# Attention and two mixture layers in one kernel: sixth unit multiplied as loaded, w_out decoded into PSUM and its logits taken from the split parts

## The chip, the core and the metric

One core of one Trainium2 chip. The metric is the device time of one execution in microseconds (us). The kernel before took 819.07 us, the median of three runs (817.53 to 819.14).

## What is computed

Sparse attention over 4 batches of 8 heads, 768 positions of 64 (a window of 128 and four leading positions), then a dense layer with a softmax-weighted activation and a layer norm, then a gated layer in which each of the 3,072 tokens goes to one of eight experts. Cut to what bears on the change:

```python
x = attn_out.transpose(0, 2, 1, 3).reshape(B * S, H * D)
h = x @ w_in
sm = softmax(h)
solu = h * sm
ln = (solu - mu) / np.sqrt(var + 1e-06) * g_ln
x2 = ln @ w_out
logits = x2 @ w_gate
expert_idx = argmax(logits); out = gate_w * (relu(x2 @ w1[e]) @ w2[e])
```

The inputs come in double precision as far as `w_in` and `w_out` are concerned: the kernel receives them as pairs of 32-bit words and makes float32 out of them itself.

## The kernel before, in words

All matrix products that need more than the short multiplication format are made from two parts: a high part (float32r, rounded by the write) and a low part (the value less its high part), so that a product takes three matmuls of one pass, or two where one side is exact.

**Attention** (`a_load`, `a_split`, `a_scores`, `a_sinks`, `a_trans`, `a_out`) runs over 32 units; a unit is two heads by 384 positions. Units 0 to 4 (`n < NATP`, NATP = 5) are multiplied as loaded: L225 multiplies float32 q and k of 64 rows directly. From unit 5 on, `a_split` makes high and low parts first: ScalarE copies k and q (L190, L191), GpSimd subtracts (L192, L193), and nine transfers on SyncE's queue (L198) stack high and low parts in the 128 rows; L228 and L229 then multiply. For each of six score tiles VectorE applies the mask and takes the maximum (L232, L233) and ScalarE the exponential (L235). The score tiles `s`, the sink tiles `skp` and, for later units, `tp` and `av` share three PSUM banks (tag "psa", PA = 3); everything else shares the other five ("psm").

**Weights** (`load_w_in`, `load_w_out`, both through `decode`) come in 16 chunks, eight of each matrix. ScalarE turns the low words into numbers (L350), VectorE joins the words in two operations (L351 into a PSUM tile `dt`, L352 into the result), ScalarE makes the high part (L362 or L397) and VectorE the low part (L363 or L398). For `w_in` the result of L352 is a PSUM tile `dh`; for `w_out` it is the SBUF tile `dec`. Each chunk of `w_out` also gives the gate's logits columns: TensorE transposes the decoded chunk in four pieces (L376), ScalarE copies it to `xt` (L378), TensorE multiplies by the gate's weights (L384, 8 columns), and VectorE writes the eight result columns behind the chunk's 512 (L387, L388). At step k of the loop the product of chunk k-2 stands ahead of the transposes of chunk k-1.

**Dense layer** (`m_in`, `m_act`, `m_tr`, `m_out`, `m_route`) runs over 24 blocks of 128 tokens. `m_in` multiplies by `w_in` (L453 to L455, 512 columns) and needs the outputs `bxh`, `bxl` (L311, L312) of four units, the first four for block 0.

**Order.** The program writes the steps in an order of its own: attention alone until the first four units are out, then attention and dense layer in a proportion (RATIO) of their estimated PE times, which the `yield` values give. The loading of weights is one step for each entry of `W_AT`: entry i says after which exponential step i comes. What is left of it is run through before the first `m_out` ("wo"). From this written order a scheduler sets each engine's own order; every engine then works its list strictly from the top.

```python
            if last2:
                logits2(*last2)
                last2 = None
            if last:
                last2 = logits(*last)
            last = (k, x)
            yield 1.5
```

Of the kernel before, what the change touches and what calls it, by code (L numbers as in the profile page):

```python
# [8 lines left out]
F32 = mybir.dt.float32  # L9
F32R = mybir.dt.float32r  # L10
BF16 = mybir.dt.bfloat16
I32 = mybir.dt.int32
U32 = mybir.dt.uint32
AF = mybir.ActivationFunctionType
ALU = mybir.AluOpType
# [14 lines left out]
NPT, XBUFS, QKB, PKB, VB = 2, 8, 2, 2, 2  # L30
WB, DB, EB, NXR, XGB = 4, 4, 2, 2, 6
PA = 3
NATP, LEAD = 5, 4
KLV = 2
LA = 2
TE = 18
# [1 line left out]
XT = 21  # L38
WSB = 6
HG, HD, HSTEP, FH = 1, 5, 2, 1  # L40
W_AT, RATIO = [1, 4, 7, 10, 13, 16, 19, 22, 24, 26, 27, 29, 30, 32, 33, 35], 0.7
ROOM = [608, 576, 512, 416, 384, 320, 288, 128]
CAPS = [-(-n // 128) * 128 for n in ROOM]
NBLK = sum(CAPS) // 128
# [4 lines left out]
SC_IN, SC_OUT, SX = 2.0 ** 8, 2.0 ** 64, 2.0 ** -8  # L49
# [3 lines left out]
def raw(ap):  # L53
    return ap.bitcast(F32)
# [3 lines left out]
def body(ctx, tc, a):  # L58
    nc = tc.nc
    V, A, G, T, SY = nc.vector, nc.scalar, nc.gpsimd, nc.tensor, nc.sync  # L60
# [3 lines left out]
    const = ctx.enter_context(tc.tile_pool(name="const", bufs=1))  # L64
# [18 lines left out]
    def ps(name):  # L83
        if name in ATT:
            a_ = True
        elif name in MOE:
            a_ = False
        else:
            flip[0] += 1
            a_ = flip[0] % 8 < PA  # L90
        return ps_p.tile([128, 512], F32, tag="psa" if a_ else "psm", name=name, bufs=PA if a_ else 8 - PA)
# [4 lines left out]
    ident = const.tile([128, 128], F32, name="ident")  # L96
# [45 lines left out]
    def in_win(out, r, tmp):  # L142
# [7 lines left out]
                           op1=ALU.mult)  # L150
# [165 lines left out]

    g_sb = const.tile([128, 8], F32, name="g_sb")
    g_s = const.tile([128, 8], F32, name="g_s")
    g_l = const.tile([128, 8], F32, name="g_l")
    wg_sb = const.tile([128, 4, NE], F32, name="wg_sb")  # L320

    dec_p = [at]

    def dec_tile(name):
        return dec_p[0].tile([128, 512], I32, tag="dec", name=name, bufs=DB)

    ex, pin = [], [None]
# [38 lines left out]

    def load_w_out(flush=False):
        sc = SC_OUT * (1.0 if flush else RAW)
        V.tensor_scalar(out=g_s, in0=g_sb, scalar1=sc, scalar2=None, op0=ALU.mult)
        V.tensor_scalar(out=g_l, in0=g_sb, scalar1=1.0 / SC_OUT, scalar2=None, op0=ALU.mult)  # L370

        def logits(k, x):

            t = ps("wt")
            for d in range(4):
                T.transpose(t[:, 128 * d:128 * d + 128], x[:, 128 * d:128 * d + 128], ident)  # L376
            xt = dec_tile("xt").bitcast(F32).rearrange("p (a b) -> p a b", a=4)
            A.activation(out=xt, in_=t.rearrange("p (a b) -> p a b", a=4), func=AF.Copy, scale=sc)  # L378
            return k, xt

        def logits2(k, xt):
            t = ps("wt2")
            for d in range(4):
                T.matmul(t[:, 0:NE], xt[:, d, :], wg_sb[:, d, :], start=(d == 0), stop=(d == 3))  # L384
            wp = t[:, 0:NE]
            gk = g_l[:, k:k + 1]
            V.tensor_scalar(out=woh[:, k, 0, 256:264], in0=wp, scalar1=gk, scalar2=None, op0=ALU.mult)  # L387
            V.scalar_tensor_tensor(out=wol[:, k, 0, 256:264], in0=wp, scalar=gk, in1=raw(woh)[:, k, 0, 256:264],  # L388
                                   op0=ALU.mult, op1=ALU.subtract)

        last = last2 = None
        for k in range(8):
            x = dec_tile("dec").bitcast(F32)
            decode(a["w_out"].bitcast(I32)[128 * k:128 * k + 128, :], x, flush)
            h_ = woh[:, k, :, 0:256]
            p2 = x.rearrange("p (a b) -> p a b", a=2)
            A.activation(out=h_, in_=p2, func=AF.Copy, scale=g_s[:, k:k + 1])  # L397
            V.scalar_tensor_tensor(out=wol[:, k, :, 0:256], in0=p2, scalar=g_s[:, k:k + 1], in1=raw(h_),  # L398
                                   op0=ALU.mult, op1=ALU.subtract)
            if last2:  # L400
                logits2(*last2)
                last2 = None
            if last:
                last2 = logits(*last)
            last = (k, x)
            yield 1.5
        logits2(*last2)
        logits2(*logits(*last))


    tri = const.tile([128, 128], BF16, name="tri")
# [871 lines left out]
    def weights():  # L1283
        yield from load_w_in()
        yield from load_w_out()
# [35 lines left out]
    wn = [0]  # L1321

    def weigh():
        while wn[0] < 16 and len(ex) > W_AT[wn[0]]:
            pin[0] = ex[W_AT[wn[0]]]
            step(gw, "w")
            wn[0] += 1
# [4 lines left out]
    while done_x[0] < 0:  # L1332
        step(ga, "a")
        cnt_ += 1
        if cnt_ == 12:
            late_loads()
        weigh()
# [4 lines left out]
    while True:  # L1342
        if a_open and ta <= tm * RATIO:
            d = step(ga, "a")
# [7 lines left out]
        d = step(gm, "m")  # L1352
# [7 lines left out]
        else:  # L1360
            d = step(ga, "a")
# [61 lines left out]
```

## Time and profile before

| | |
|---|---|
| median of three runs | 819.07 us (817.53 to 819.14) |
| the profiled execution's own time | 819.58 us |
| its span from first to last instruction | 817.4 us |
| mean granted TensorE clock, share of full speed | 0.985 |
| TensorE matmul busy | 776.4 us, 95% of the span |
| VectorE busy | 478.5 us, 59% |
| ScalarE busy | 461.9 us, 57% |
| GpSimd busy | 355.4 us, 43% |

A span is counted from the first instruction; an execution's own time is 2.2 us longer here. The shares are means over the whole kernel: the first tenth, where the units before the dense layer and the decoding of the weights lie, looks unlike the rest and is read by itself.

### The profile page before, as it was taken

What the parts mean: (1) busy time and instruction counts of PE and PEld (TensorE: products, weight loads), DVE (VectorE), ACT (ScalarE), POOL (GpSimd) and SP (SyncE); (2) the same over time, 40 slices, a digit from 0 to 9 for tenths busy, and PEclk for the clock granted to TensorE, in tenths of its full rate; (3) what the DMA queues carried; (4) which work ended last, traced back from release to release, by engine and by line L of the source; (5) the groups of instructions that cost most, each with busy time, mean ns of one, the idle gap of its engine ahead of it and who ended that gap; (6) DMA issues with size and microseconds to landing.
All of it is one profiled execution on the core that took longest, in us unless ns stands there. A gap on an engine that the chain in (4) does not pass through costs nothing.

```text
span 817.4 us, 15512 instructions
## 1 busy us (share of the span) xinstructions
PE 776.4 (95%) x5003; PEld 670.3 (82%) x5003; DVE 478.5 (59%) x1766; ACT 461.9 (57%) x1236; POOL 355.4 (43%) x393
## 2 busy tenths in 40 slices
PE   4779999999999998999999998999999999999996
PEld 2457788897988887888988898888978888989885
DVE  6898666676758647766776566426333443435541
ACT  3677686675757848657766374235425243436442
POOL 3565354545354544555433121156235244535533
PEclk9968999999999999999999999999999999999998
DMA  8585355567557457474530271195375416663650
GB/s 272 186 260 155 92 150 119 131 135 142 126 132 156 117 113 161 121 154 102 142 85 27 32 239 44 46 330 204 101 254 193 156 63 213 225 211 96 227 172 28
DMA packets 78281, 120.82 MB, mean 148 GB/s; under 512 B 14122, under 2 KB 52524, under 8 KB 78192
## 3 DMA queue, kind: packets, MB, share of 16 engines
q1 hardware_dynamic: 70512, 97.48, 44.5%
q0 software_dynamic: 5088, 13.88, 4.8%
q10 hardware_dynamic: 2592, 8.39, 3.0%
q8 instruction: 42, 0.69, 0.4%
q14 instruction: 47, 0.39, 0.2%
HBM read 80.61 MB, written 13.28 MB: 115 GB/s over the span
## 4 chain that ended last, share of the span: by engine, by line
PE 78%; DVE 9%; DMA 5%; issue 3%; ACT 2%; POOL 1%; POOLq 0%; SPq 0%; ACTq 0%; DVEq 0%
PE ht L853 6%; PE ht L854 6%; PE ht L852 6%; PE x L523 5%; PE y L922 5%; PE h L453 5%; PE y L924 5%; PE y L923 5%; PE x L525 5%; PE x L524 5%; PE h L454 5%; PE av L306 4%; PE h L455 4%; PE s L228 3%; PE s L229 2%
## 5 line engine op out<-in xcount | busy, mean ns | idle before, releaser
L523 PE MATMUL x<-woh,lh 128*128 128x264 f32 (+1 forms) x384 | 111.5, 290 | 0.1
L525 PE MATMUL x<-woh,ll 128*128 128x264 f32 (+1 forms) x384 | 109.5, 286 | 0.0
L524 PE MATMUL x<-wol,lh 128*128 128x264 f32 (+1 forms) x384 | 109.0, 284 | 0.0
L235 ACT ACTIVATE P<-P,mx 128x144 f32<-128x144 f32 x192 | 78.5, 411 | 49.3 <-DVE mx L233 46.9
L760 ACT ACTIVATE wh<-wst 128x1024 fp32r<-128x1024 f32 x64 | 67.5, 1058 | 45.9 <-PE ht L853 26.6
L768 POOL TENSOR_TENSOR wl<-wst,wh 128x1024 fp32r<-128x1024 f32 x28 | 67.8, 2423 | 55.1 <-ACT wh L760 48.1
L853 PE MATMUL ht<-xel,wh 128*128 128x288 f32 (+5 forms) x256 | 81.2, 318 | 0.0
L854 PE MATMUL ht<-xeh,wl 128*128 128x288 f32 (+5 forms) x256 | 81.0, 318 | 0.0
L453 PE MATMUL h<-wih,bxh 128*128 128x512 f32 x192 | 79.0, 412 | 1.0 <-DVE ll L506 0.9
L768 DVE TENSOR_TENSOR wl<-wst,wh 128x1024 fp32r<-128x1024 f32 x36 | 53.1, 1478 | 45.9 <-ACT wh L760 44.0
L852 PE MATMUL ht<-xeh,wh 128*128 128x288 f32 (+5 forms) x256 | 79.7, 318 | 0.0
L922 PE MATMUL y<-wh,hh 128*128 128x512 f32 x192 | 77.2, 402 | 1.2 <-DVE hl L861 1.2
L454 PE MATMUL h<-wil,bxh 128*128 128x512 f32 x192 | 76.4, 398 | 0.0
L924 PE MATMUL y<-wh,hl 128*128 128x512 f32 x192 | 75.5, 395 | 0.0
L923 PE MATMUL y<-wl,hh 128*128 128x512 f32 x192 | 75.2, 392 | 0.0
L455 PE MATMUL h<-wih,bxl 128*128 128x512 f32 x192 | 74.3, 399 | 0.0
L523 PEld LDWEIGHTS x<-woh,lh 128*128 128x128 f32 x384 | 72.4, 188 | 1.7 <-DVE r L556 0.3
L232 DVE COPY_PREDICATED s<-pick,s 128x128 f32<-128x128 int32 x160 | 45.2, 292 | 48.6 <-PE s L229 45.9
L524 PEld LDWEIGHTS x<-wol,lh 128*128 128x128 f32 x384 | 72.4, 189 | 0.7
L525 PEld LDWEIGHTS x<-woh,ll 128*128 128x128 f32 x384 | 72.3, 189 | 0.6 <-issue 0.3
L193 POOL TENSOR_TENSOR lA<-qd,qA 128x384 fp32r<-128x384 f32 x27 | 28.1, 1042 | 95.3 <-ACT qA L191 75.0
L244 POOL TENSOR_TENSOR pk<-P,sm 128x768 f32<-128x768 f32 x32 | 47.6, 1487 | 45.2 <-DVE sm L242 38.8
(275 smaller groups left out, 2046.5 us busy)
## 6 DMA issues: line engine op xcount, KB each, us to landing
wst<-w SPq DMA_DIRECT2D x64, 512.0 KB
x_d<-xrow SPq DMA_DIRECT2D x24, 264.0 KB
qd<-qT SPq DMA_DIRECT2D x32, 192.0 KB
qB<-qA SPq DMA_DIRECT2D x54, 96.0 KB
lB<-lA SPq DMA_DIRECT2D x54, 96.0 KB
kd<-kx SPq DMA_DIRECT2D x16, 280.0 KB
w<-w_in ACTq DMA_DIRECT2D x8, 512.0 KB
w<-w_out ACTq DMA_DIRECT2D x8, 512.0 KB
```

The costliest lines, as they stand in the source:

```text
L453: T.matmul(h, xh[k], wih[:, k, cs], start=(k == 0), stop=False)
L454: T.matmul(h, xh[k], wil[:, k, cs], start=False, stop=False)
L523: T.matmul(p[:, 0:n], lh[:, k, :], woh[:, k, c, 0:n], start=(k == 0), stop=False)
L524: T.matmul(p[:, 0:n], lh[:, k, :], wol[:, k, c, 0:n], start=False, stop=False)
L525: mm = T.matmul(p[:, 0:n], ll[:, k, :], woh[:, k, c, 0:n], start=False, stop=(k == 7))
L768: return (G if c % 2 and r else V).tensor_tensor(out=l_, in0=st_w.pop((r, which, c)), in1=raw(h_), op=ALU.subtract)
L852: T.matmul(o, wh[:, k, fs], xh(k), start=(k == 0), stop=False)
L853: T.matmul(o, wh[:, k, fs], xl(k), start=False, stop=False)
L854: T.matmul(o, wl[:, k, fs], xh(k), start=False, stop=(k == 3))
L922: T.matmul(o, hh[:, k, sl], wh, start=(k == 0), stop=False)
L923: T.matmul(o, hh[:, k, sl], wl, start=False, stop=False)
L924: T.matmul(o, hl[:, k, sl], wh, start=False, stop=(k == 7))
```

## The change

Three parts. NATP goes from 5 to 6, so unit 5 is multiplied as loaded and `a_split` starts with unit 6. The chunks of `w_out` are decoded into PSUM (`dh`), as those of `w_in` were, and the logits are taken from the finished high and low parts: eight float32r matmuls of 128 columns against an identity, accumulated in pairs, take the place of four float32 transposes, and `xt` then holds the scaled weights, so that the factor per row in L387 and L388 falls away. The product with the gate's weights follows one chunk later (LAG = 3), which makes the loop eleven steps long; `W_AT` has three more entries for them.

```diff
-NATP, LEAD = 5, 4
+NATP, LEAD = 6, 4
+LAG = 3
-W_AT, RATIO = [1, 4, 7, 10, 13, 16, 19, 22, 24, 26, 27, 29, 30, 32, 33, 35], 0.7
+W_AT, RATIO = [1, 4, 7, 10, 13, 16, 19, 22, 24, 26, 27, 29, 30, 32, 33, 35, 37, 38, 40], 0.7
...
-        V.tensor_scalar(out=g_l, in0=g_sb, scalar1=1.0 / SC_OUT, scalar2=None, op0=ALU.mult)
+        ident_r = dec_p[0].tile([128, 128], F32R, tag="idr", name="ident_r")
+        V.tensor_copy(ident_r, ident)
-        def logits(k, x):
+        def logits(k):
             t = ps("wt")
             for d in range(4):
-                T.transpose(t[:, 128 * d:128 * d + 128], x[:, 128 * d:128 * d + 128], ident)
+                for n, w in enumerate((woh, wol)):
+                    T.matmul(t[:, 128 * d:128 * d + 128], w[:, k, d // 2, 128 * (d % 2):128 * (d % 2) + 128], ident_r,
+                             start=(n == 0), stop=(n == 1))
             xt = dec_tile("xt").bitcast(F32).rearrange("p (a b) -> p a b", a=4)
-            A.activation(out=xt, in_=t.rearrange("p (a b) -> p a b", a=4), func=AF.Copy, scale=sc)
+            A.activation(out=xt, in_=t.rearrange("p (a b) -> p a b", a=4), func=AF.Copy)
...
-            gk = g_l[:, k:k + 1]
-            V.tensor_scalar(out=woh[:, k, 0, 256:264], in0=wp, scalar1=gk, scalar2=None, op0=ALU.mult)
+            V.tensor_scalar(out=woh[:, k, 0, 256:264], in0=wp, scalar1=1.0 / SC_OUT, scalar2=None, op0=ALU.mult)
...
-        for k in range(8):
-            x = dec_tile("dec").bitcast(F32)
-            decode(a["w_out"].bitcast(I32)[128 * k:128 * k + 128, :], x, flush)
+        done = []
+        for k in range(8 + LAG):
+            if k < 8:
+                x = decode(a["w_out"].bitcast(I32)[128 * k:128 * k + 128, :], None, flush)
...
+            if k >= LAG:
+                logits2(*done.pop(0))
+            if 0 < k < 9:
+                done.append(logits(k - 1))
             yield 1.5
-        logits2(*last2)
-        logits2(*logits(*last))
```

In the changed kernel the lines are numbered anew: L398 becomes L400, L397 L399, L376 L378, L378 L381, L384 L387, L387 and L388 become L389 and L390, L225 is L226, L272 is L273, L453 to L455 are L451 to L453.

VectorE's list, from the decoding of the first `w_out` chunk to the sink tile `skt` of units 2 and 3. Before:

```order
L351 SCALAR_TENSOR_TENSOR dt<-w_569 128x512
L363 SCALAR_TENSOR_TENSOR wil<-dh,wih 128x512
L352 SCALAR_TENSOR_TENSOR dec<-w_569,dt 128x512
L351 SCALAR_TENSOR_TENSOR dt<-w_590 128x512
L398 SCALAR_TENSOR_TENSOR wol<-dec,g_s,woh 128x2x256
L312 SCALAR_TENSOR_TENSOR bxl<-wt,bxh 128x384
L232 COPY_PREDICATED s<-pick,s 128x128
L352 SCALAR_TENSOR_TENSOR dec<-w_590,dt 128x512
L232 COPY_PREDICATED s<-pick,s 128x128
L398 SCALAR_TENSOR_TENSOR wol<-dec,g_s,woh 128x2x256
L387 TENSOR_SCALAR woh<-wt_598,g_l 128x8
L272 TENSOR_TENSOR skt<-skp,skt 128x384
```

Now:

```order
L352 SCALAR_TENSOR_TENSOR dh<-w_549,dt 128x512
L351 SCALAR_TENSOR_TENSOR dt<-w_568 128x512
L313 SCALAR_TENSOR_TENSOR bxl<-wt,bxh 128x384
L352 SCALAR_TENSOR_TENSOR dh<-w_568,dt 128x512
L233 COPY_PREDICATED s<-pick,s 128x128
L400 SCALAR_TENSOR_TENSOR wol<-dh,g_s,woh 128x2x256
L351 SCALAR_TENSOR_TENSOR dt<-w_593 128x512
L233 COPY_PREDICATED s<-pick,s 128x128
L273 TENSOR_TENSOR skt<-skp,skt 128x384
```

Ahead of `skt` stand two low parts of `w_out` before and one now; the third chunk's L352 and the first logits column (L387) now come behind it.

TensorE's list, from the sink transposes of units 2 and 3 and the last scores of unit 4 to the transposes of unit 3's weights (`pk`). Before:

```order
L270 MATMUL skp<-ident,psk 128x128 x3
L225 MATMUL s<-kd,qd 128x272 x2
L384 MATMUL wt_598<-wg_sb,xt 128x8 x4
L376 MATMUL wt<-ident,dec 128x128 x4
L228 MATMUL s<-kA,qA 128x272
...
L384 MATMUL wt_641<-wg_sb,xt 128x8 x4
L376 MATMUL wt<-ident,dec 128x128 x4
L284 MATMUL wt<-ident,pk 128x128 x6
```

Now:

```order
L271 MATMUL skp<-ident,psk 128x128 x3
L226 MATMUL s<-kd,qd 128x272 x2
L378 MATMUL wt<-ident_r,woh 128x128
L378 MATMUL wt<-ident_r,wol 128x128
...
L226 MATMUL s<-kd,qd 128x272 x2
L387 MATMUL wt_642<-wg_sb,xt 128x8 x4
...
L285 MATMUL wt<-ident,pk 128x128 x6
```

Ahead of L387 stand two pairs of L226 of unit 5 (the second is shown), where L228 stood; between them and ahead of L285 stand the logits matmuls of three chunks (24 rows, alternately from `woh` and `wol`) and the product of one.

## Rows read from the trace of the kernel before

**Rows 1.** The page's part 1: busy time, share of the span, instructions.

```profile
PE 776.4 (95%) x5003; PEld 670.3 (82%) x5003; DVE 478.5 (59%) x1766; ACT 461.9 (57%) x1236; POOL 355.4 (43%) x393
```

**Rows 2.** Busy time of each engine in stretches of 10 us: busy us (x instructions), then PEclk, DMA share, GB/s.

```profile
40.00:50.00 10.00, 7.79 (x42) 5.08 (x43) 9.37 (x30) 9.13 (x26) 6.87 (x8) 0.83 0.86 245
50.00:60.00 10.00, 6.59 (x34) 6.24 (x34) 8.89 (x25) 5.52 (x14) 7.44 (x7) 0.60 0.93 279
...
70.00:80.00 10.00, 8.27 (x52) 7.52 (x51) 8.35 (x28) 4.93 (x15) 3.58 (x5) 0.79 0.43 110
...
110.00:120.00 10.00, 10.00 (x85) 9.20 (x84) 5.45 (x30) 7.03 (x24) 6.19 (x8) 1.00 0.56 147
```

**Rows 3.** TensorE alone in the three stretches at half clock, same columns.

```profile
41.86:45.06 3.20, 3.20 (x12) 0.50 0.74 192
51.98:62.10 10.12, 7.70 (x34) 0.50 0.88 248
75.93:82.40 6.47, 6.28 (x24) 0.50 0.17 39
```

**Rows 4.** Timeline of TensorE, 50 to 55 us: start, us, engine, line, out<-in, [idle before <-releaser].

```profile
50.35 0.63 PE L376 MATMUL wt<-ident,dec 128*128 128x128 f32 x4
54.40 0.57 PE L228 MATMUL s<-kA,qA 128*128 128x272 f32 x1 [3.41 <-issue]
```

**Rows 5.** Timeline of VectorE, 49 to 55 us.

```profile
49.88 1.21 DVE L398 SCALAR_TENSOR_TENSOR wol<-dec,g_s,woh 128x512 fp32r<-128x512 f32 x1
...
51.67 0.68 DVE L352 SCALAR_TENSOR_TENSOR dec<-w,dt 128x512 int32<-128x512 int32 x1
...
52.47 1.23 DVE L398 SCALAR_TENSOR_TENSOR wol<-dec,g_s,woh 128x512 fp32r<-128x512 f32 x1
53.62 0.21 DVE L387 TENSOR_SCALAR woh<-wt,g_l 128x8 fp32r<-128x8 f32 x1
53.76 0.54 DVE L272 TENSOR_TENSOR skt<-skp,skt 128x384 fp32r<-128x384 f32 x1
```

**Rows 6.** Low parts, by line: count, then ns min/median/max, first and last start.

```profile
L398 DVE SCALAR_TENSOR_TENSOR wol<-dec,g_s,woh x8: 739/790/1595, 49.9 to 81.1; 128x512 fp32r<-128x512 f32 x8
L363 DVE SCALAR_TENSOR_TENSOR wil<-dh,wih x8: 676/684/691, 13.8 to 47.7; 128x512 fp32r<-128x512 f32 x8
```

**Rows 7.** Timeline of TensorE: first units as loaded, later ones split.

```profile
38.60 1.18 PE L225 MATMUL s<-kd,qd 64*128 64x272 f32 x6
...
63.28 0.29 PE L228 MATMUL s<-kA,qA 128*128 128x272 f32 x1
63.40 0.29 PE L229 MATMUL s<-kA,lA 128*128 128x272 f32 x1
```

**Rows 8.** GpSimd's part of a split unit, by line: as rows 6.

```profile
L192 POOL TENSOR_TENSOR kd<-kd,kA x27: 1068/1369/1844, 40.2 to 408.1; 128x560 fp32r<-128x560 f32 x15, 128x416 fp32r<-128x416 f32 x12
L193 POOL TENSOR_TENSOR lA<-qd,qA x27: 993/1014/1447, 41.5 to 405.5; 128x384 fp32r<-128x384 f32 x27
```

**Rows 9.** Timeline of TensorE: short matmuls at full clock, four kinds.

```profile
49.44 1.06 PE L384 MATMUL wt<-wg_sb,xt 128*128 128x8 f32 x8
...
211.84 0.60 PE L502 MATMUL lt<-ident,e 128*128 128x128 f32 x4
...
543.87 0.28 PE L854 MATMUL ht<-xeh,wl 128*128 128x224 f32 x1
543.98 0.27 PE L852 MATMUL ht<-xeh,wh 128*128 128x224 f32 x1
```

**Rows 10.** Timeline of VectorE and TensorE: last output of unit 3, and who needs it.

```profile
68.69 0.52 DVE L312 SCALAR_TENSOR_TENSOR bxl<-wt,bxh 128x384 fp32r<-128x384 f32 x1
...
69.64 0.39 PE L453 MATMUL h<-wih,bxh 128*128 128x512 f32 x1
```

**Rows 11.** Timeline of TensorE: waits for the logits' copies.

```profile
73.82 1.06 PE L384 MATMUL wt<-wg_sb,xt 128*128 128x8 f32 x8 [0.51 <-ACT xt L378]
...
76.12 1.87 PE L384 MATMUL wt<-wg_sb,xt 128*128 128x8 f32 x8 [0.75 <-ACT xt L378]
```

More of the change, by code (lines that the diff above doesn't have):

```diff
@@ L318, in body @@
     g_s = const.tile([128, 8], F32, name="g_s")
-    g_l = const.tile([128, 8], F32, name="g_l")
     wg_sb = const.tile([128, 4, NE], F32, name="wg_sb")
@@ L385, in logits2 @@
             wp = t[:, 0:NE]
-            gk = g_l[:, k:k + 1]
-            V.tensor_scalar(out=woh[:, k, 0, 256:264], in0=wp, scalar1=gk, scalar2=None, op0=ALU.mult)
-            V.scalar_tensor_tensor(out=wol[:, k, 0, 256:264], in0=wp, scalar=gk, in1=raw(woh)[:, k, 0, 256:264],
-                                   op0=ALU.mult, op1=ALU.subtract)
-        last = last2 = None
-        for k in range(8):
-            x = dec_tile("dec").bitcast(F32)
-            decode(a["w_out"].bitcast(I32)[128 * k:128 * k + 128, :], x, flush)
[L395 to L400, printed above, removed]
-                logits2(*last2)
[L402 to L405, printed above, removed]
+            V.tensor_scalar(out=woh[:, k, 0, 256:264], in0=wp, scalar1=1.0 / SC_OUT, scalar2=None, op0=ALU.mult)
+            V.scalar_tensor_tensor(out=wol[:, k, 0, 256:264], in0=wp, scalar=1.0 / SC_OUT,
+                                   in1=raw(woh)[:, k, 0, 256:264], op0=ALU.mult, op1=ALU.subtract)
+        done = []
+        for k in range(8 + LAG):
+            if k < 8:
+                x = decode(a["w_out"].bitcast(I32)[128 * k:128 * k + 128, :], None, flush)
+                h_ = woh[:, k, :, 0:256]
+                p2 = x.rearrange("p (a b) -> p a b", a=2)
+                A.activation(out=h_, in_=p2, func=AF.Copy, scale=g_s[:, k:k + 1])
+                V.scalar_tensor_tensor(out=wol[:, k, :, 0:256], in0=p2, scalar=g_s[:, k:k + 1], in1=raw(h_),
+                                       op0=ALU.mult, op1=ALU.subtract)
+            if k >= LAG:
+                logits2(*done.pop(0))
+            if 0 < k < 9:
+                done.append(logits(k - 1))
             yield 1.5
-        logits2(*last2)
-        logits2(*logits(*last))
     tri = const.tile([128, 128], BF16, name="tri")
@@ L1323, in weigh @@
     def weigh():
-        while wn[0] < 16 and len(ex) > W_AT[wn[0]]:
+        while wn[0] < len(W_AT) and len(ex) > W_AT[wn[0]]:
             pin[0] = ex[W_AT[wn[0]]]
```

## The prediction

> **What bounds the kernel now.** I read the page's part 1 first, then the busy times by stretches of 10 us, then the timelines of TensorE and VectorE where a stretch stands out. Over the whole span TensorE is busy 95% [rows 1], so from the point where it never waits again, every us of its work is a us of time. The stretches say where that point lies: at 110 to 120 us TensorE is busy all 10 us at full clock, at 40 to 60 and at 70 to 80 it is not [rows 2]. Nothing that the change adds or takes away comes later than about 110 us, so the early stretch decides. There VectorE is the fullest engine (9.37 of 10 us at 40 to 50, 8.89 at 50 to 60) [rows 2], and TensorE loses time in two ways. It waits: 3.4 us up to 54.40 [rows 4], and 0.51 and 0.75 us for the logits' copies [rows 11]. And its granted clock is halved, 1.2 GHz in place of 2.4, three times, with 3.20, 7.70 and 6.28 us of busy time in those stretches [rows 3]; half of that is lost, 3.85 us in the second and 3.14 in the third. The third follows directly on the waits of 72 to 76 us, where TensorE is busy 8.27 of 10 us [rows 2, 11].
>
> Why the long wait ends when it does: the profile calls it "issue", which names nobody. But the matmul that starts at 54.40 [rows 4] needs one of the three score banks, and the one freed last is that of the sink tile, which VectorE's L272 finishes reading at 53.76 + 0.54 = 54.30 [rows 5]. It was not waiting for the split of unit 5. L272 stood in VectorE's list behind the decoding of w_out, two low parts of 1.2 us among it [rows 5].
>
> And what starts the dense layer: its first block needs the output of unit 3, whose low part is written at 68.69 to 69.21; the matmul on it starts at 69.64 [rows 10]. Until then TensorE is not the bound, and work put on it there costs only what it delays unit 3.
>
> **The change part by part.** The sum is made against the profiled execution's own 819.58 us (span 817.4 and 2.2 around it); the median of the runs shown, 819.07, lies 0.5 lower.
>
> *Low parts from PSUM.* L398 reads two SBUF tiles and takes 739 to 1595 ns; L363, the same operation with its first input in PSUM, takes 676 to 691 [rows 6]. L398 differs also in its factor per row, so 0.68 to 0.74 us bound the new one; I take 0.68, since tile, shape and engine are the same. In the two in front of L272 that is 1.21 - 0.68 = 0.53 us each [rows 5].
>
> *The new order of VectorE's list.* Ahead of the sink tile one low part (1.2), one L352 (0.68) and one L387 (0.21) move behind it [rows 5]. With 0.53 for the low part that stays, the sink tile is read 2.6 us earlier. What moved still has to be done before unit 3's output, so of the 2.6 only the shorter low parts (five of them ahead of that output, two at 0.53, three near the short end at 0.1) and one L387 with its L388 (0.4) are saved for good there: 1.8 us. But TensorE's wait of 3.4 us, which VectorE paid for with waits of its own on the scores, shrinks too. I take unit 3's output **2.0 us earlier** (0 if TensorE's own list is last there, 3.4 if the whole wait counts).
>
> *Unit 5 as loaded.* Six matmuls of two records each take 2.4 us by the six records in 1.18 us; the twelve split ones took 1.4 by their spacing of 0.12 [rows 7]. The 1.0 more lies before unit 3's output, in the place of the 3.4 us wait, and costs nothing if that cover holds. Removed are two copies on ScalarE, two subtractions on GpSimd (1.37 and 1.01 us [rows 8]) and nine transfers on SyncE's queue. None of them ended a wait of TensorE: I cost them at nothing. The loads of unit 5 now go into unit 3's buffers and so wait for unit 3's scores; these end about 40 us, over 10 us before unit 5 is multiplied.
>
> *The logits.* 32 transposes become 64 matmuls of 128 columns. A transpose costs (0.60 - 0.27) / 3 = 0.11 us at full clock, so all 32 take 3.5 us [rows 9]. No row shows a float32r matmul of 128 columns; the nearest, 224 columns, start 0.11 us apart, barely less than 272 columns, which start 0.12 apart [rows 7, 9], so the load of the weights and not the columns sets it there. From below 0.11 is bounded by little, say half, if short matmuls overlap as nothing here does; from above by the float32 matmul of 8 columns with its two records, (1.06 - 0.26) / 7 x 2 = 0.23 [rows 9]. I take 0.11, the nearest row. Four of eight chunks come before unit 3's output and fill waits; for the four behind it 32 x 0.11 - 16 x 0.11 = **+1.8 us** (0 to +5.6).
>
> The Trainium skill ("TensorE: Matmul & The Clock Gate", section on the back-to-back issue gap) gives about 81 ns for each matmul of 128 columns in a stream with its weight loads. By that the four late chunks would add 0.8 us rather than 1.8, and the median would come to 815.0, an estimate from that page. No run shown has such a matmul; the spacing of 0.11 is measured, on wider ones, and stays.
>
> *One chunk of lag.* In TensorE's new list, whole groups of the dense layer's matmuls stand between a chunk's transposition and its product, where before the product of two chunks came with almost nothing between. The two waits of 0.51 and 0.75 us [rows 11] go: **-1.3 us** (0 if others take their place). The third stretch at half clock follows on them; I take half of its 3.14 us as gone, **-1.6 us** (0 to -3.1), because other waits of that stretch stay and the clock fell three times in 40 us.
>
> *ScalarE.* The high part from PSUM is no slower than from SBUF by any row; ScalarE is busy 5.52 of 10 us at 50 to 60 [rows 2] and hides it. If that cover were gone the change would still be a tenth of a us for each chunk.
>
> Sum: -2.0 + 1.8 - 1.3 - 1.6 = -3.1; 819.58 - 3.1 = 816.5, and 0.5 lower as a median: **816.0 us**.
>
> **The rivals.** About 0.2%, 1.6 us, is what a measurement of this kernel can tell from no change.
>
> A. *Both later stretches at half clock go.* With the wait before 54.40 filled by logits matmuls, the clock stays up, TensorE reaches unit 3's transposes earlier, and the whole 3.4 us count; the third stretch saves 3.1. For it: the list now has matmuls in the wait. Against it: the fall at 51.98 came only 1 us after the wait began, and a shorter wait is left. Sum -3.4 + 1.8 - 1.3 - 3.1 = -6.0: 813.1.
>
> B. *TensorE is last before unit 3's output.* If the clock falls as before, 24 logits matmuls at twice 0.11 are 5.3 us of work ahead of unit 3's transposes, and the dense layer starts no earlier; the third stretch stays too. Sum 0 + 1.8 - 1.3 = +0.5: 819.6, no difference that can be told.
>
> C. *Slower: a matmul of 128 columns costs as much as the float32 ones, 0.23.* Then the four late chunks cost 32 x 0.23 - 1.8 = 5.6, and the early ones 32 x 0.12 = 3.8 more than taken, which turns the 2.0 won into 1.8 lost, and the clock is not helped. Sum 1.8 + 5.6 - 1.3 = +6.1: 825.2. It decides from 0.21 us a matmul on, where the late chunks alone eat 4.9 us. Against it: 224 columns show no such step.
>
> D. *The banks.* The chunks decoded after the dense layer has begun now hold two of the five other banks, where they held one, from L352 to the low part. That is two operations of 0.68 and ScalarE's copy between, about 2 us a chunk; if the dense layer's matmuls wait half of that in four chunks, +4.0: 816.0 + 4.0 = 820.0. For it: five banks serve h, transposes and decoding alike. Against it: w_in was decoded so throughout, with TensorE no worse off.
>
> **How the numbers follow.** Forecast 0.42, A 0.15, B 0.18, C 0.10, D 0.15. Faster by over 0.2% are the forecast nearly whole, A, and a little of D: 0.57. Within 0.2% are most of B and half of D: 0.21. Slower are C, the rest of B and of D: 0.22. For the range, A's 813.1 with one us for what the scheduler moved elsewhere gives 812.0; the other end takes in B and D with the same us: 821.0. C is left out, and some of A.
>
> **What would show it.** Right: the matmul of unit 5's first scores starts at 52 to 53 us, the wait before it is under 1.5 us; every low part of w_out takes 0.68 to 0.74 us; unit 3's low part is written before 67.5; logits matmuls start 0.11 apart at full clock; no wait on `xt` over 0.3 us. Wrong: unit 3's output comes at 69 us or later (B), the spacing is near 0.23 (C), or matmuls of the dense layer wait for VectorE's reads of `dh` (D). The forecast as a whole is wrong if TensorE's idle time and half-clock time before 110 us together are no smaller than before, or if waits of another kind appear behind 110 us.

## The result, and the profile after

The changed kernel takes **830.27 us**, the median of four runs (829.30 to 833.63), against 819.11 for the kernel before beside it: a ratio of 1.0145, 95% interval 1.0112 to 1.0179. Six more runs on another occasion gave 826.47 (825.06 to 832.84), ratio 1.0118 (1.0089 to 1.0146). It is slower by 1.2 to 1.5%; the forecast was 816.0, the range ended at 821.0. The profiled execution took 830.94 us; its span is 829.2, 11.8 longer than that of before.

The page's part 1, engine, busy us, share of the span, instructions, as [rows 1]:

```profile
PE 784.5 (95%) x5035; PEld 675.3 (81%) x5035; DVE 475.8 (57%) x1766; ACT 460.3 (56%) x1234; POOL 351.1 (42%) x391
```

TensorE is busy 8.1 us longer (a matmul at half clock counts with its longer time), and every other engine less. The stretches of 10 us of the changed kernel, TensorE's busy us (instructions), granted clock, DMA share and GB/s, to be read beside [rows 2]; then its three half-clock stretches, beside [rows 3]:

```profile
40.00:50.00 10.00, 6.17 (x34) 0.90 0.67 234
50.00:60.00 10.00, 9.08 (x36) 0.50 0.87 239
60.00:70.00 10.00, 10.00 (x63) 0.75 0.45 126
70.00:80.00 10.00, 10.00 (x66) 1.00 0.54 149
110.00:120.00 10.00, 10.00 (x77) 1.00 0.26 78
190.00:200.00 10.00, 7.33 (x39) 0.83 0.51 92
...
47.92:64.99 17.07, 15.93 (x66) 0.50 0.73 213
194.69:198.10 3.41, 2.93 (x10) 0.50 0.38 84
495.06:498.47 3.41, 3.41 (x18) 0.50 0.90 294
```

The stretch at 75.93 is gone, as hoped, but the clock falls earlier, at 47.92, and stays at half for 17 us; and there are two new stretches late in the program, where before had none between 82 us and the last 5. The one at 194.69 lies in a stretch in which TensorE is idle 2.67 us.

TensorE's timeline of the changed kernel where [rows 4] and [rows 10] stood, and the logits matmuls at full clock (start, us, engine, line, out<-in, [idle before <-releaser]):

```profile
47.56 0.60 PE L271 MATMUL skp<-ident,psk 128*128 128x128 f32 x3 [2.38 <-POOL psk L254]
...
50.41 0.47 PE L378 MATMUL wt<-ident_r,wol 128*128 128x128 f32 x1 [0.63 <-DVE wol L400]
50.68 0.41 PE L378 MATMUL wt<-ident_r,woh 128*128 128x128 f32 x1
50.90 0.41 PE L378 MATMUL wt<-ident_r,wol 128*128 128x128 f32 x1
...
52.89 1.51 PE L226 MATMUL s<-kd,qd 64*128 64x272 f32 x4 [0.51 <-PE wt L378]
...
69.05 0.27 PE L378 MATMUL wt<-ident_r,woh 128*128 128x128 f32 x1
69.17 0.28 PE L378 MATMUL wt<-ident_r,wol 128*128 128x128 f32 x1
```

The 3.41 us of [rows 4] are gone. A logits matmul starts 0.11 to 0.12 us after the one ahead of it at full clock and 0.21 to 0.22 at half, and 24 of the 64 stand in the stretch at half. The clock's fall at 47.92 comes right behind a new wait, 2.38 us for the weights of the sink columns (`psk`, GpSimd). VectorE's timeline has the output of unit 3, at 68.69 in [rows 10], at 70.33:

```profile
70.33 0.52 DVE L313 SCALAR_TENSOR_TENSOR bxl<-wt,bxh 128x384 fp32r<-128x384 f32 x1
```

The low parts of `w_out` by line, as [rows 6], take 0.74 to 0.75 us, where before had up to 1.60:

```profile
L400 DVE SCALAR_TENSOR_TENSOR wol<-dh,g_s,woh x8: 736/750/751, 49.6 to 79.7; 128x512 fp32r<-128x512 f32 x8
```

Where the time went. Three long stretches of TensorE (busy us, then as above), of before and of the changed kernel:

```profile
0.00:110.00 110.00, 87.01 (x433) 0.91 0.64 190
110.00:300.00 190.00, 187.72 (x1349) 1.00 0.60 135
300.00:540.00 240.00, 232.40 (x1600) 1.00 0.45 112
```

```profile
0.00:110.00 110.00, 89.73 (x475) 0.92 0.59 178
110.00:300.00 190.00, 181.50 (x1278) 0.99 0.61 133
300.00:540.00 240.00, 232.02 (x1616) 0.99 0.43 102
```

Up to 110 us TensorE is idle 20.3 us, 2.7 less than before. From 110 to 300 it is idle 8.5, where before it was 2.3. The experts' matmuls `ht<-xeh,wh` mark two points that follow the same work in both kernels; the line gives count, ns min/median/max, first and last start. Before, then the changed kernel:

```profile
L852 PE MATMUL ht<-xeh,wh x256: 264/302/392, 543.1 to 783.1; 128*128 128x288 f32 x48, 128*128 128x224 f32 x16, 128*128 128x512 f32 x16, 128*128 128x416 f32 x16
```

```profile
L850 PE MATMUL ht<-xeh,wh x256: 268/302/397, 552.8 to 794.1; 128*128 128x288 f32 x48, 128*128 128x224 f32 x16, 128*128 128x512 f32 x16, 128*128 128x416 f32 x16
```

So 9.7 of the 11.8 us are lost before the experts' stage, 1.3 in it (241.3 for 240.0) and 0.8 behind it. The 9.7 are made up thus: idle -2.7 + 6.2 + 0.4 = +3.9; time lost to the clock, half of the busy time at half clock, (15.93 + 2.93 + 3.41) / 2 = 11.1 against (3.20 + 7.70 + 6.28) / 2 = 8.6 [rows 3], +2.5; 32 more matmuls at 0.11, +3.5. Together 9.9; the 1.0 us that the prediction gives unit 5's scores as loaded is not in it, so the sum is good to about 1 us. The clock's part is that of these two executions: noscat_b (below), which runs as before does up to the first scatter, has its clock at half from about 29 to 39 us, where before has not.

The waits of TensorE between 110 and 260 us (line and what it waited for: total, times, longest), before:

```profile
PE tp L284 <- ACT pt L285: 0.9, 1, 0.9
PE tp L284 <- DVE skt L272: 0.5, 1, 0.5
PE h L453 <- DVE ll L506: 0.3, 1, 0.3
```

and in the changed kernel, then the longest of them in its timeline:

```profile
PE s L230 <- DMA lA<-lA: 5.0, 3, 2.7
PE tp L285 <- ACT pt L286: 1.0, 1, 1.0
```

```profile
195.17 0.59 PE L230 MATMUL s<-kA,lA 128*128 128x272 f32 x1 [2.67 <-DMA lA<-lA]
```

`lA` is the low part of q in a split unit; a transfer on SyncE's queue copies it to the other 64 rows (`a_split`). The clock's fall at 194.69 lies in that wait.

### The profile page after: what moved, and what is told of

The parts are those of the page before. It is cut to its first block, busy times and chain, and to the rows that moved or that the text cites. A ratio compares the mean times of both kernels' runs of the same rounds, so it can differ in the third digit from the quotient of the medians.

```text
span 829.2 us, 15566 instructions
## 1 busy us (share of the span) xinstructions
PE 784.5 (95%) x5035; PEld 675.3 (81%) x5035; DVE 475.8 (57%) x1766; ACT 460.3 (56%) x1234; POOL 351.1 (42%) x391
## 4 chain that ended last, share of the span: by engine, by line
PE 77%; DMA 8%; DVE 7%; issue 3%; ACT 2%; POOL 1%; SPq 1%; POOLq 0%; ACTq 0%; DVEq 0%
PE ht L850 6%; PE ht L852 6%; PE ht L851 6%; PE y L920 5%; PE y L922 5%; PE y L921 5%; PE x L521 5%; PE x L523 5%; PE x L522 5%; PE h L451 5%; PE h L452 4%; PE h L453 4%; PE av L307 4%; DMA lA<-lA 3%; PE s L229 2%
## 5 line engine op out<-in xcount | busy, mean ns | idle before, releaser
L521 PE MATMUL x<-woh,lh 128*128 128x256 f32 (+1 forms) x384 | 111.5, 290 | 1.2 <-ACT lh L503 1.1
L522 PE MATMUL x<-wol,lh 128*128 128x256 f32 (+1 forms) x384 | 109.7, 286 | 0.0
L766 DVE TENSOR_TENSOR wl<-wst,wh 128x1024 fp32r<-128x1024 f32 x36 | 55.2, 1534 | 51.9 <-ACT wh L758 51.8
L451 PE MATMUL h<-wih,bxh 128*128 128x512 f32 x192 | 78.8, 411 | 1.2 <-DVE ll L504 1.2
L453 PE MATMUL h<-wih,bxl 128*128 128x512 f32 x192 | 74.4, 398 | 0.0
```

The source lines that it names most:

```text
L451: T.matmul(h, xh[k], wih[:, k, cs], start=(k == 0), stop=False)
L521: T.matmul(p[:, 0:n], lh[:, k, :], woh[:, k, c, 0:n], start=(k == 0), stop=False)
L522: T.matmul(p[:, 0:n], lh[:, k, :], wol[:, k, c, 0:n], start=False, stop=False)
L766: return (G if c % 2 and r else V).tensor_tensor(out=l_, in0=st_w.pop((r, which, c)), in1=raw(h_), op=ALU.subtract)
```

## Experiments

The diffs are against the kernel that each sentence names. Ratios are to the kernel before, run beside each set.

### One edit at a time

`NATP` does three things: unit 5 is multiplied as loaded, `a_split` starts later, and, since the pace that a unit's scores declare hangs on the same number, unit 5 declares 0.45 for 0.23. The first two go together; with the pace and the `w_out` part that makes three edits, each on or off, in eight kernels.

natp6, against before:

```diff
-NATP, LEAD = 5, 4
+NATP, LEAD = 6, 4
```

> The kernel before with one part of the change alone: six units are multiplied as loaded instead of five, and w_out is decoded and its logits are made as before. Theory 1 (order: with six raw units the scheduler brings the attention later against the dense layer, and TensorE then waits for the loads of late units, 5.0 us at the reload of the sink tile in the changed kernel): most of the 11.2 us appear here, 825 to 830 us, with over 3 us of waits for that load between 129 and 250 us. Theory 2 (the w_out part: 32 matmuls more at 0.11 us, its decode through PSUM, its later logits): at or below the kernel before, 815 to 820 us. Theory 3 (scatter: any change of the order moves this kernel by several us, through chance meetings of loads and their users): anywhere from 814 to 828 us.

wout5, against the changed kernel:

```diff
-NATP, LEAD = 6, 4
+NATP, LEAD = 5, 4
```

> The changed kernel with five raw units again: all of the w_out part, none of the sixth unit. Theory 1 (order by the sixth unit): back to the kernel before plus the extra matmuls, 819 to 823 us. Theory 2 (the w_out part): 827 to 831 us. Theory 3 (scatter): anywhere from 816 to 830 us, and the waits behind 110 us are for other loads than in the changed kernel.

pace_b, against before:

```diff
-                yield 0.45 if n < NATP else 0.23
+                yield 0.45 if n < NATP + 1 else 0.23
```

> A control: the kernel before, with nothing but the pace changed that the sixth unit's scores declare to the scheduler (0.45 for 0.23), so that the same instructions stand in a slightly different order (dense layer against scores) and no work is added. Theories 1 and 2: 819 us within 2 us, since the attention does not fall behind for long. Theory 3 (scatter): off by more than 4 us to either side, with new waits between 110 and 500 us.

pace_a, against the changed kernel (r_only is the same edit to natp6, pw is pace_b's edit to wout5):

```diff
-                yield 0.45 if n < NATP else 0.23
+                yield 0.45 if n < NATP - 1 else 0.23
```

> The same control on the changed kernel: the sixth unit declares 0.23 for 0.45, every instruction is kept. Theory 1: a smaller lag of the attention, 825 to 830 us. Theory 2: 830 us within 2 us. Theory 3 (scatter): off by more than 4 us to either side, the waits for the sink tile's load gone or moved to another place.

> The sixth unit multiplied as loaded and nothing else: its scores declare the old 0.23, w_out as before. With the other runs it completes a table of three edits (raw unit, pace, w_out), each on or off. Theory A (the edits add up, the w_out part costs what it costs): the raw unit alone is worth +3 to +4 us, as between the two kernels with the new pace (811.25 and 815.01), so 822 to 823 us. Theory B (chance meetings of loads and their users after 110 us decide): not additive, off by more than 3 us from 822.5 to either side.

> The w_out part and the new pace, five raw units. Theory A (additive): the w_out part adds what it adds to the kernel before (825.84 against 819.92, 6 us), the pace takes 8.7: 817 to 818 us. Theory B (chance): off by more than 3 us. In both the wait of TensorE for the psk tile at about 47 us stays at 2.4 to 2.7 us and the clock is at half for some 14 us behind it, since that goes with the w_out part in every run so far.

The expectations call the transfer `lA<-lA` the load of the sink tile, wrongly; and "scatter" in Theory 3 means chance, not the scatter of token ids that comes further down. The medians are of different occasions, so they are compared by their ratios. Measured:

| raw unit | pace | w_out part | kernel | median us | ratio (95%) | waits for `lA`, 110 to 430 us |
|---|---|---|---|---|---|---|
| - | - | - | before | 819.11 | 1 | 0.8 |
| - | yes | - | pace_b | 811.25 | 0.9912 (0.9879 to 0.9944) | 0.7 |
| yes | - | - | r_only | 818.86 | 1.0026 (1.0001 to 1.0050) | 1.7 |
| yes | yes | - | natp6 | 815.01 | 0.9935 (0.9910 to 0.9960) | 1.6 |
| - | - | yes | wout5 | 825.84 | 1.0075 (1.0045 to 1.0105) | none |
| - | yes | yes | pw | 821.45 | 1.0037 (1.0021 to 1.0053) | 0.9 |
| yes | - | yes | pace_a | 833.39 | 1.0168 (1.0103 to 1.0233) | 3.1 |
| yes | yes | yes | the change | 830.27 | 1.0145 (1.0112 to 1.0179) | 5.0 |

The sixth unit with its pace makes the kernel faster, by 0.65%, so Theory 1 falls. The `w_out` part costs 0.75% by itself and 2.1% on top of the sixth unit and its pace: it is the part that loses, as Theory 2 has it, but not by its own work alone. pace_b meets the condition of Theory 3: a number that only tells the scheduler how long a step is, with no work changed, is worth 0.88%, 7 us.

r_only and pw miss the sums of Theory A, which are in us, by 3 to 4 us to opposite sides, but those sums go by the kernel before of an earlier occasion (819.92; beside r_only and pw it took 817.92). In ratios r_only is where the sum has it (0.9935 / 0.9912 = 1.0023, measured 1.0026), and pw is 0.5% above it (1.0075 x 0.9912 = 0.9987). So raw unit and pace add up; what does not add up is the `w_out` part with either. The rest is regular, though steps of 0.2 to 0.4% are hardly clear of their intervals: the raw unit costs 0.2 to 0.3% without the `w_out` part and 0.9 to 1.1% with it, at either pace; the pace saves 0.9% without it and 0.2 to 0.4% with it; and the waits for `lA` are longest where raw unit and `w_out` part are both. They are not the whole loss: wout5 has none of them and costs 0.75% all the same.

### The first stretch

whwh, against the changed kernel:

```diff
-                for n, w in enumerate((woh, wol)):
+                for n, w in enumerate((woh, woh)):
```

> The changed kernel, its logits from the high part twice in place of high and low: as many matmuls, of the same size, but none waits for the low part; the logits leave the low parts out. If it is the wait for the low part that takes the first block's logits out of the gap ahead of the psk tile: the wait at 47 us falls from 2.4 to 1.4 us or less, the half-clock stretch behind it shortens, and the total is 823 to 827 us. If the block's decode itself comes too late for that gap (it begins at 47.9 us on VectorE where it was 45.9), nothing changes there: 2.4 us and 828 to 832 us.

decsb, against the changed kernel:

```diff
-                x = decode(a["w_out"].bitcast(I32)[128 * k:128 * k + 128, :], None, flush)
+                x = dec_tile("dec").bitcast(F32)
+                decode(a["w_out"].bitcast(I32)[128 * k:128 * k + 128, :], x, flush)
```

> The changed kernel, but w_out is decoded into an SBUF tile as before, and the parts are taken from there; the logits stay as changed. If the PSUM tile ties the first block's decode to the buffers of w_in's decode: the decode moves ahead to 46 us, the wait for the psk tile falls below 2 us, and the low parts cost 0.79 us and more again; 824 to 829 us. If the extra matmuls and the order behind 110 us are what costs: 829 to 833 us, and the MoE stage (the last 305 us) stays some 2 us longer than in the kernel before.

whwh: 825.64 us, ratio 1.0113 (1.0056 to 1.0171), the wait for `psk` still 2.4 us: it is not the low part that keeps the logits out of that gap. decsb: 825.17 us, ratio 1.0114 (1.0076 to 1.0151). Its wait for `psk`, and its stretches of 10 us:

```profile
PE skp L271 <- POOL psk L254: 0.9, 1, 0.9
```

```profile
50.00:60.00 10.00, 9.73 (x38) 0.51 0.83 243
60.00:70.00 10.00, 10.00 (x47) 0.63 0.31 108
```

So the PSUM tile does tie the first chunk's decode to that of `w_in` and opens the wait, but the clock is at half just as long without it. The wait is not what the change loses its time by, and neither run can be told from the changed kernel's second set (1.0118).

### Thirty-two bytes

In every run of the first sets with the `w_out` part the experts' stage was longer than in those without. One line of the change, which the prediction never looked at, takes away a tile of 32 bytes:

```diff
-    g_l = const.tile([128, 8], F32, name="g_l")
```

In the compiled program the tiles allocated behind it move down by 32 bytes (`wih` from byte 24992 of each partition to 24960, `xeh` from 84768 to 84736), while the expert weights, in a pool on the other side, stay. The attention's own tiles lie 512 bytes lower, since the new `ident_r` takes that much of their pool; no run undoes that. gl allocates the tile of 32 bytes again, used by nothing; the streams of instructions stay the same on all five engines:

```diff
-    g_s = const.tile([128, 8], F32, name="g_s")
+    g_s = const.tile([128, 8], F32, name="g_s"); const.tile([128, 8], F32, name="g_l")
```

> The changed kernel with the 32-byte tile g_l, which the change dropped, allocated again and used by nothing: every engine's stream of instructions is the same, and the tiles that lie behind it in SBUF (the dense layer's weights, bxh, xeh, hh and so on) are back at their old addresses, 32 bytes on. If the addresses are what makes the MoE stage longer in every run with the w_out part (the matmuls of L920 to L922 at 407, 395 and 397 ns where the kernels without it have 403, 392 and 394): the span from the 24th block's end falls by 1.5 to 2.5 us, and the total is 827.5 to 829 us. If not: 830 us within 1.5.

after2 and gl2 are the changed kernel and gl once more, beside each other:

> The changed kernel itself once more, beside the three others on one chip, so that its difference to the kernel with g_l allocated is measured there. If the 9 us between 830.27 and 821.02 are the addresses and no difference between chips: 828 to 832 us, a ratio to the kernel before of 1.012 to 1.017.

> The changed kernel with g_l allocated, again, on the chip of the run above. Addresses (theory G): 819 to 823 us, 7 us or more below the changed kernel. If only the MoE stage answers to the addresses (its length went from 299.2 to 295.5 us in the two profiles) and the rest was chance: 3 to 5 us below it.

bshift, against before, is the converse (the factor is written over `g_sb`, which nothing reads afterwards here):

```diff
-    g_l = const.tile([128, 8], F32, name="g_l")
+    g_l = g_sb
```

> The converse on the kernel before: g_l is written in place of g_sb, so that its 32-byte tile is gone and the tiles behind lie 32 bytes lower, as in the changed kernel; instructions and their order are those of the kernel before. Theory G: the MoE stage 3 to 4 us longer, 821 to 824 us; if the earlier stages answer to the addresses too, up to 828 us. If it takes the changed kernel's other parts for the addresses to matter: 818 to 820 us.

Measured: gl 821.02 us, ratio 1.0033 (1.0009 to 1.0057); after2 826.47, 1.0118 (1.0089 to 1.0146); gl2 822.07, 1.0048 (1.0028 to 1.0068); bshift 822.68, 1.0058 (1.0042 to 1.0074). The experts' matmuls `y` by line (count, busy us, mean ns), changed kernel:

```profile
L920 PE MATMUL y<-wh,hh 128*128 128x512 f32 x192 | 77.9, 406 | 1.2 <-DVE hl L859 1.2
L922 PE MATMUL y<-wh,hl 128*128 128x512 f32 x192 | 76.0, 397 | 0.0
L921 PE MATMUL y<-wl,hh 128*128 128x512 f32 x192 | 75.8, 395 | 0.0
```

The same three of gl, then the stage in gl and in bshift, by the line that marked it above:

```profile
L920 PE MATMUL y<-wh,hh 128*128 128x512 f32 x192 | 77.2, 402 | 1.2 <-DVE hl L859 1.2
L922 PE MATMUL y<-wh,hl 128*128 128x512 f32 x192 | 75.5, 395 | 0.0
L921 PE MATMUL y<-wl,hh 128*128 128x512 f32 x192 | 75.2, 392 | 0.0
```

```profile
L850 PE MATMUL ht<-xeh,wh x256: 264/302/392, 547.1 to 785.5; 128*128 128x288 f32 x48, 128*128 128x224 f32 x16, 128*128 128x512 f32 x16, 128*128 128x416 f32 x16
```

```profile
L852 PE MATMUL ht<-xeh,wh x256: 268/302/398, 545.0 to 786.4; 128*128 128x288 f32 x48, 128*128 128x224 f32 x16, 128*128 128x512 f32 x16, 128*128 128x416 f32 x16
```

The stage lasts 238.4 us in gl and 241.3 in the changed kernel, 2.9 us for the same matmuls, each some ns longer; bshift, the kernel before with the lower addresses, has 241.4. (Before's own 240.0 holds a pause on another line, L907, whose matmuls `y<-wst,hr` are busy 12.7 us there and 11.7 in these three, with 0.7 idle. The pause goes with the set of runs rather than with the kernel: natp6, pace_b, wout5 and pace_a of the first set and mend and pace_defer of the last have it, the twelve profiles between have not. It stays unexplained. Without the pause the stage lasts 238.3 or 238.4 us in every kernel with the tile and 241.3 or 241.4 in every one without it; with the pause, 240.0 to 240.2 and 243.0 to 243.3.) The addresses are shown to cost the kernel before 0.58%, 4.7 us. In the changed kernel they are worth 4.4 us beside each other (826.47 against 822.07) and 9.2 across occasions, so gl's expectation was too small, and the 9.2 too large; the profiles show 2.9 in the stage, and the rest lies ahead of it, in waits and clock that differ between executions. How far the addresses cause that rest stays open.

### The scatter of token ids

The last instruction of a block's routing (`m_route`) is a scatter by GpSimd: 128 token ids of 4 bytes, to places in `id_d`. One of the changed kernel's three waits for `lA` ends at 137.03:

```profile
137.03 0.39 PE L230 MATMUL s<-kA,lA 128*128 128x272 f32 x1 [1.73 <-DMA lA<-lA]
```

What was issued between 122 and 126 us, and between 184 and 187.4 (count, KB each, median us to landing):

```profile
lB<-lA SPq DMA_DIRECT2D x2, 96.0 KB, 2.2
...
lA<-lA SPq DMA_DIRECT2D x1, 96.0 KB, 11.7
id_d<-tok_i,si POOLq DMA_INDIRECT x1, 12.5
...
kB<-kA SPq DMA_DIRECT2D x1, 140.0 KB, 8.6
```

A copy of a size that takes 2.2 us elsewhere is issued at 125.29, 2.7 us after the scatter, and lands at 137.0, 1.9 us after it. The trace of before holds no landing times of its copies; that of bshift, which has before's order, does. From 100 to 300 us its `lA` copies take 2.1 us at the median and its `kB<-kA` copies of 140 KB 5.9, the changed kernel's 7.7 and 5.1 (of those copies whose landing is recorded). So late copies are in both, and late copies of `lA` in the changed order. noscat, against the changed kernel, and noscat_b, against before, leave the scatter of the first 16 blocks out:

```diff
-        i = G.indirect_dma_start(out=id_d, out_offset=bass.IndirectOffsetOnAxis(ap=si[:, 0:1], axis=0),
+        i = None if t < 16 else G.indirect_dma_start(out=id_d, out_offset=bass.IndirectOffsetOnAxis(ap=si[:, 0:1], axis=0),
                                 in_=ids, in_offset=None)
```

> The changed kernel without the scatter of token ids of the first 16 token blocks (the routing's last instruction; those ids are left out, so that the experts later gather other tokens). The order on TensorE and VectorE stays but for a few rows. Theory S (the scatter takes 6 to 12 us to land, and the transfers of a unit's parts that are issued just behind it land no sooner; the sixth raw unit moved the splits into its way): the 5.0 us of waits for lA (which the earlier expectations call the sink tile, wrongly: it is the low part of q) fall under 1.5 us, the clock's fall at 194.7 us goes with them, 822 to 826 us. Theory B (order, the splits are late on ACT and POOL): the waits stay above 3 us and the time at 829 to 832 us.

> The same left out of the kernel before, whose waits for lA are 0.8 us in all. Theory S: there is little to gain, 817 to 819 us (at most 1.5 us). Theory B: the same, 818 to 820. A gain above 3 us would mean that the scatter costs the kernel before as much, and that its meeting with the splits is no difference between the two.

gl_noscat is noscat with gl's tile:

> The changed kernel with g_l allocated and without the scatter of the first 16 token blocks (their ids are left out). If addresses and scatter are two causes that add up: 9 and 11 us off 830 together, 809 to 812 us, which is below the kernel before without its scatter (814.65) or level with it. If both act through the same thing (the chance by which the transfers of lA land in time): 814 to 819 us, hardly below either alone.

Measured: noscat 818.64 us, ratio 1.0004 (0.9986 to 1.0022); noscat_b 814.65, 0.9953 (0.9936 to 0.9970); gl_noscat 815.80, 0.9975 (0.9960 to 0.9989). noscat's waits for `lA` are gone (its copies take 2.1 and 2.4 us at the median), and what it issued between 122 and 126 us:

```profile
lB<-lA SPq DMA_DIRECT2D x2, 96.0 KB, 2.2
vd<-vp SPq DMA_DIRECT2D x1, 192.0 KB, 2.6
...
lA<-lA SPq DMA_DIRECT2D x1, 96.0 KB, 2.1
```

The scatter costs the changed kernel 1.1 to 1.4%, 9 to 12 us, more than Theory S asked. It costs the kernel before 0.47%, 3.9 us, which is more than the 1.5 us of Theory S, and more than the 3 us from which, as the expectation has it, the scatter costs both alike. It does not: 3.9 us are common to both kernels, and 5 to 8 come on top in the changed one. Where the 3.9 lie in the kernel before is not shown. The profiles give 2.3 us ahead of the experts' stage (its first matmul at 540.8 for 543.1), 0.8 of them before's wait for `lA`, but with more half clock in noscat_b's; the other 1.6 (238.4 for 240.0) are the pause, which kernels with every scatter lack too.

With the scatter out of both, the changed kernel is 0.51% slower (1.0004 against 0.9953); with the old addresses as well, 0.22% (0.9975 against 0.9953), 1.8 us. gl_noscat lies in the range of its second answer: 0.29% under noscat, while gl lies 0.7 to 1.1% under the changed kernel, so part of what the addresses seemed to cost goes with the scatter. The same holds the other way round: with the old addresses the scatter costs the changed kernel 0.58 to 0.73% (1.0033 and 1.0048 against 0.9975), little more than the kernel before. The 5 to 8 us thus belong to scatter and lower addresses together. Nor are they the waits for `lA` alone: decsb waits 0.6 us for `lA` in its profile and has the ratio 1.0114.

### Mending it, and a version better than both

pace_c, against before:

```diff
-                yield 0.45 if n < NATP else 0.23
+                yield 0.45 if n < NATP + 3 else 0.23
```

> The kernel before with the pace 0.45 declared by three more units (the sixth to the eighth) and nothing else; a search for a version better than both, along the one edit that made the kernel faster (the sixth unit alone: 811.25 us). If a slower pace of the attention early on helps by itself: 808 to 813 us. If the gain at the sixth unit was one of order by chance: 814 to 822 us.

mend (the changed kernel with gl's tile) and pace_defer (pace_b) keep the places of 19 blocks and scatter them together:

```diff
-        V.tensor_copy(si, s_)
-        i = G.indirect_dma_start(out=id_d, out_offset=bass.IndirectOffsetOnAxis(ap=si[:, 0:1], axis=0),
-                                 in_=ids, in_offset=None)
+        c0 = min(pend + [t])
+        if main and t < TE:
+            pend.append(t)
+        else:
+            V.tensor_copy(si_all[:, c0:t + 1], s_all[:, c0:t + 1])
+            for c in range(c0, t + 1):
+                i = G.indirect_dma_start(out=id_d, out_offset=bass.IndirectOffsetOnAxis(ap=si_all[:, c:c + 1], axis=0),
...
```

> The changed kernel with both causes mended and nothing left out: g_l allocated again, and the token ids of the first 19 blocks scattered together after the 19th block, when the attention is over (19 scatters in a row on POOL). Theory (addresses and the meeting of scatter and splits are what the change costs): the waits for lA below 1 us, 814 to 818 us, as without the scatter (815.8), unless the late scatters make the first expert's token ids late: then a new wait at 480 to 500 us, up to 10 us, and 818 to 828 us.

> A search for a version better than both kernels: the kernel before with the new pace (811.25 us) and the ids of the first 19 blocks scattered together after the 19th block. If the scatter costs this kernel as much as the kernel before (3.9 us): 806 to 809 us. If it costs it little, since its waits for lA are 0.7 us: 809 to 812 us. If the ids then come too late for the first expert: 812 to 822 us with a new wait at 480 to 500 us.

pace_c: 818.10 us, ratio 1.0000 (0.9977 to 1.0023), and 4.1 us of waits for `lA`: the gain of one slower unit is not a rule of slower pacing. mend: 850.08, ratio 1.0384 (1.0357 to 1.0411); pace_defer: 843.59, 1.0305 (1.0282 to 1.0329). Both misses are in the place that the expectations named, and far larger. TensorE's last scores on `lB` in noscat, then in mend, and mend's waits from 440 to 560 us:

```profile
L230 PE MATMUL s<-kB,lB x78: 282/288/296, 74.9 to 433.1; 128*128 128x272 f32 x78
```

```profile
L230 PE MATMUL s<-kB,lB x78: 282/288/297, 74.3 to 432.4; 128*128 128x272 f32 x78
```

```profile
PE x L522 <- ACT lh L504: 12.8, 1, 12.8
PE xt L818 <- DMA xg<-x_d,idx_i: 10.6, 1, 10.6
```

Up to the end of the attention mend, which leaves nothing out, is as quick as noscat: its last scores start at 432.4 and 433.1 us, and it has no wait for `lA`. In gl, which scatters after each block and is otherwise nearly the same, they start at 439.0, in the changed kernel at 442.0. So the gain comes from the scatters being elsewhere, and not from the ids that noscat leaves out. What mend saves there, 9.6 us against the changed kernel, it loses three times over behind it (its span is 848.2 us for 829.2), where 19 scatters and the first experts' loads come together. The best kernel stays **pace_b, 811.25 us**, 0.9% below the kernel before and 2.3% below the changed one.

## Why the prediction was wrong

**The step that failed first: "Nothing that the change adds or takes away comes later than about 110 us, so the early stretch decides."** The change adds nothing there, but it moves the order of the split units against the dense layer and the scatters, and it moves the tiles. Of the 11.8 us of the two profiles, 6.2 are idle time between 110 and 300 us and 2.1 lie in and behind the experts' stage. The runs show what it costs: with the tile of 32 bytes allocated again and nothing left out, the change costs 0.3 to 0.5% in place of 1.2 to 1.5; with the scatter out of both kernels, 0.51%; with both, 0.22%, 1.8 us. The two overlap, and how the 5 to 8 us divide that only the changed kernel loses to the scatter at its lower addresses stays open. That this order meets the scatters more often than pace_b's is seen in the waits; no run shifts the scatters a little against the copies. The sentence in the test list held: waits of another kind did appear behind 110 us.

**The removed work, costed "at nothing".** Right for the engines that the text names. But the nine transfers were weighed only as something taken away. The units that are still split, from unit 6 on, have the same nine, and their landing was not looked at, nor what else is in flight beside them. The pace that hangs on NATP was not seen at all; alone it is worth -7 us, so what the rest costs is more than the change shows (2.1% on top of natp6).

**The logits, "+1.8".** The price was right and the place wrong. 0.11 us for a matmul of 128 columns is what the rows at 69 us show; rival C's 0.23 is seen at half clock alone. But 24 of them ran there, ahead of unit 3's transposes, which is the first half of rival B. The 81 ns of the Trainium skill ("TensorE: Matmul & The Clock Gate", section on the back-to-back issue gap) are not reached in those rows (0.11 us and more).

**The new order of VectorE's list, "2.0 us earlier".** Unit 3's output came 1.6 us later, 70.33 for 68.69, though unit 5's scores started at 52.89, inside the 52 to 53 named, with a wait of 0.51. The long wait went as said. The time it gave back went into the matmuls at half clock: rival B's condition, "If the clock falls as before".

**The lag, "-1.3" and "-1.6".** No wait for `xt` is left, and the third half-clock stretch went whole. In its place stand a longer one, from 47.92, and two falls behind 110 us.

**Low parts from PSUM, 0.68.** 0.75 at the median, just above the bound of 0.74; that is 0.07 us more in each of eight chunks. decsb, which decodes into SBUF, has single ones of 1.9.

So to 110 us the change is near rival B's +0.5 (idle -2.7, clock 15.93 / 2 - 8.6 = -0.6, matmuls +3.5, together +0.2), against a forecast of -3.1; with gl's tile and without the scatter it is +1.8 us in all. The other 8 to 10 us came from where the range allowed "one us for what the scheduler moved elsewhere".

## What to carry to other kernels

Where a scheduler or a pool allocator stands between the edit and the program, list what it moved in the whole program, instructions and tile addresses, before calling any stretch untouched; a control that changes only the order, or only an address, tells how large that is (here 7 us and 4.7 us). Price an edit on a kernel this full against the spread of such controls, not against zero. Where copies feed the bounding engine, look at what their queue neighbours do to their landing.

## What the runs showed of the hardware

- Two programs with the same streams of instructions, whose tiles lie 32 bytes apart, differ by 2.9 us in the experts' stage: `y` matmuls of 512 columns take 406 and 395 ns instead of 402 and 392. The faster ones have `hh` and `xeh` at an odd multiple of 32 bytes (24992 and 84768), the slower ones at a multiple of 64 (24960 and 84736); which of the tiles it is was not tried.
- In the changed kernel scatters of 128 ids of 4 bytes took 5.5 to 12.5 us to land, and the two copies of 96 and 140 KB shown beside them 11.7 and 8.6; without the scatters such copies took 2.1 and 2.4 at the median. The Trainium skill ("DMA: Bandwidth & Descriptors", Specifications) says that transfers below 512 bytes make the DMA engine read before it writes; no run here tells whether that is the reason.
- 19 scatters in a row, with the first experts' loads behind them, cost 32 us over one scatter a block (843.59 against pace_b's 811.25).
